# Down projection by seven half-size products, with the residual kept in DRAM

## The chip, the core and the metric

The kernel runs on one core of a Trainium2 chip. The metric is device time in microseconds (us), lower is better. Times shown are medians over several executions; the profile and the trace come from one execution of their own, in which the hardware profiler ran.

The core's engines each work through a queue of their own: TensorE (PE in the profile, its weight loads PEld), VectorE (DVE), ScalarE (ACT), GpSimd (POOL) and SyncE (SP). Here SP issues nearly all transfers between DRAM and the on-chip memory. TensorE writes its products to the eight banks of PSUM, from where VectorE and ScalarE fetch them.

## The reference

A transformer block with modulation: 2048 tokens of width 1024, 32 query heads over 4 key-value heads of 128, the last 512 cached keys, and a gated MLP of width 3584. All inputs are bfloat16.

```python
mod = (silu(c) @ w_mod).reshape(1, 6, 1, -1)
sa, ca, ga, sb, cb, gb = ...                     # six rows of mod
h = layernorm(x) * (1 + ca) + sa
x = x + ga * attention(h, k_cache[-512:], v_cache[-512:], wq, wo)
h = layernorm(x) * (1 + cb) + sb
x = x + gb * ((silu(h @ w_gate) * (h @ w_up)) @ w_down)
```

The last product, with `w_down` of 3584 x 1024, is the down projection. The sum in front of it is the residual.

## The kernel before

The attention works on four chunks of 512 tokens. In each chunk 32 heads are taken one by one; the query projection of a later head pair is done in seven products in place of eight (the same trick that the change uses below), its weight sums being kept in DRAM as `wq_sums` after the first chunk. A chunk ends with its output projection (`oproj`): 256 matmuls of 128x128 by 128x512 into all eight banks, in eight blocks of four heads. The weights of a block, 1 MB, lie in one of three buffers; `load_wo` loads a block's successor-but-two when the block is done. The last 64 matmuls finish the banks one after the other, and `add_to_x` (L678) multiplies each bank by the gate and adds it to `x_sb`, the residual, 32 KB in each partition and resident for the whole kernel. `oproj` calls `each` at fixed places; in the last chunk this runs pending work (the second norm, first sums of gate and up weights), in the others it does nothing.

The MLP works on two stretches of 1024 tokens (`NST`). In a stretch, 14 pairs (`NPR`) of 128-column tiles of F follow each other. `pair` (L987) makes gate and up for two tiles of F and two token halves in 14 products of four matmuls: `keep` copies a product from PSUM with ScalarE, `add` adds a later one to it with VectorE (L1003), `silu` runs on ScalarE and `times` (L1014) multiplies gate by up on VectorE. Between them `sums_of_pair` (through `tt_`, L540) makes the weight sums of the next pair, four for gate and four for up. The results lie in `gu`, 28 tiles of 1024 tokens.

Then `down` (L1067) runs twice, once for each half of the 1024 output columns: 8 token tiles x 28 tiles of F, 224 matmuls, into eight banks. Its weights come in pieces of 512 KB through six buffers (`load_wd`, issued by SP). Each finished bank goes through `add_to_x`, and `store` writes 128 KB of the output. During the first stretch's `down`, VectorE makes the norm of the second stretch, which SP transposes, and the sums of the normed input (`stretch_sums`). In the very last tile the columns are done in two parts of 256, so that only a small piece is left at the end.

Order on an engine is the order of the program. Buffers are tracked by `_Tracker`: an instruction waits on semaphores for the last writer and readers of what it touches, and `_Map.take` hands on these waits when a region of on-chip memory gets a new use. All places in the memory are written out by hand, in KB (`AT_X`, `AT_H`, ...).

Of the kernel before, what the change touches and what calls it, by code (L numbers as in the profile page):

```python
# [3 lines left out]
ALU = mybir.AluOpType  # L4
AF = mybir.ActivationFunctionType
BF16 = mybir.dt.bfloat16
# [112 lines left out]
def bass_adaLN_cond__sliding_block_cached__swiglu_ffn__prompt_kernel(  # L119
# [60 lines left out]
    x_sb = M.take(AT_X * KB, [NCH * TPC, D], BF16, BX)  # L180
# [71 lines left out]
    Q_last = [dq("q_last%d" % i) for i in range(1)]  # L252
# [6 lines left out]
    with nc.Block() as block:  # L259

        @block.gpsimd
        def _(g):
# [437 lines left out]

            def oproj(ch, first, each):
# [8 lines left out]
                for b_ in range(2, HG - 2):  # L710
                    for h in range(4 * b_, 4 * b_ + 4):
                        for k in range(TPC * HALF):
                            o_mm(ch, k, h)
                    load_wo(ch * HG + b_ + 3)
                    each()
                for k in range(TPC * HALF):
# [3 lines left out]
                    add_to_x(bank(o_bank(ch, k)), PB[o_bank(ch, k)], ga_bc, B_ga[hf], ch * TPC + tt, hf * 512, 512, k % 2)  # L720
# [35 lines left out]
            def mod_columns():  # L756

                while columns:
# [14 lines left out]
                    else:  # L773
                        T.op(DVE, lambda: V.tensor_copy(sb[:, 4 * hf:4 * hf + 4], bank(QBK, 4)), writes=PB[QBK] + [B_sb])

# [58 lines left out]
            for i in range(NA):  # L834
# [78 lines left out]
                if h == Hq - 1:  # L913
# [10 lines left out]
                    oproj(ch, o_start(ch), lambda: None)  # L924
# [5 lines left out]
            raw = [[M.take((144 + 8 * i + 4 * m) * KB, [DT, 256], BF16, [B_raw[i][m]]) for m in range(2)] for i in range(NRW)]  # L930
            Q_raw = [[dq("q_raw%d_%d" % (i, m)) for m in range(2)] for i in range(NRW)]
            B_ft = [bufs("ft%d_" % i, 4) for i in range(NTS)]
            ftq = [M.take((168 + 4 * i) * KB, [4, 4, P], F16, B_ft[i]) for i in range(NTS)]
# [3 lines left out]
            fn = [[M.take((180 + 4 * m + 2 * i) * KB, [CH], F32, [B_fn[m][i]]) for i in range(2)] for m in range(2)]  # L937
            B_gx, B_ux, B_sl = bufs("gx", 2), bufs("ux", 3), bufs("sl", 4)
            ux = [M.take((196 + i) * KB, [CH], F16, [B_ux[i]]) for i in range(3)]
            sl_ = [M.take((199 + i) * KB, [CH], F16, [B_sl[i]]) for i in range(4)]  # L940
# [46 lines left out]
            def pair(gp, order):  # L987

                p = gp % NPR
                f0, f1 = 2 * p, 2 * p + 1  # L990
# [22 lines left out]
                def times(f, half, u_, s_, bb=()):  # L1013
                    T.op(DVE, lambda: V.tensor_tensor(gu(f)[:, half * CH:(half + 1) * CH], u_[0], s_[0], ALU.mult),  # L1014
                         reads=[s_[1]] + [x for x in u_[1:]], writes=[B_gu[f]] + list(bb))

                keep(0, 1, 0)
                sums_of_pair(gp + 1, 0, 0)
                g_ = add(0, 2, one[0], 0)
                keep(1, 1, 0)  # L1020
                sl = silu(g_[0], [g_[1]], [])
                keep(0, 6, 1)
                sums_of_pair(gp + 1, 0, 1)
                u_ = add(1, 2, one[1], 0)
                times(f0, 0, u_, sl)
                keep(1, 6, 1)
                sums_of_pair(gp + 1, 0, 2)
# [175 lines left out]
```

## Time and profile before

| | |
|---|---|
| median of 9 runs | 1212.37 us (1211.81 to 1214.22) |
| the profiled execution | 1213.67 us, of which the span is 1211.9 us |
| ScalarE, copy of 128x512 float32 from PSUM (L996) | 168 of 596 ns |
| VectorE, addition from PSUM (L1003) | 168 of 689 ns |
| VectorE, gate times up, in on-chip memory (L1014) | 84 of 425 ns |
| VectorE, weight sums of 512 elements, bfloat16 and float16 in, float16 out (L540) | 224 of 418 ns |
| VectorE, gate times a bank of an output (L679) | 63 of 691 ns |
| DMA transposes | 159, median 4.3 us to landing |

The page of a profile lists the engines' busy time and its share of the span, then the span in 40 slices with a digit for each tenth of busy time, the granted TensorE clock (9 is full speed) and the DMA. "Chain" is the work that ended last, followed back from the end. Groups are instructions of one line and shape, with their number, their busy time and the mean of one. A timeline entry has start, duration, engine, line, operation, and in brackets the idle time before it and what ended that. L264 is the one line through which every matmul is issued.

### The profile page before, as it was taken

How to read it: one execution, taken by the hardware profiler on the slowest of the kernel's cores; microseconds unless marked ns; L12 is line 12 of the kernel's file. 1: busy time of each engine (PE TensorE's matmuls, PEld its weight loads, DVE VectorE, ACT ScalarE, POOL GpSimd, SP SyncE). 2: the span in 40 equal slices, each digit the busy share in tenths (PEclk: the TensorE clock that was granted, in tenths of full speed). 3: DMA queues.
4: the chain of work that ended last, by engine and by line, in shares of the span. 5: the costliest groups of instructions: out<-in, count | busy, mean ns of one | idle time of the engine just before them, and what ended most of it. 6: DMA issues, size and time to landing. Idle time of an engine off the chain costs nothing.

```text
span 1211.9 us, 20448 instructions
## 1 busy us (share of the span) xinstructions
PE 1188.8 (98%) x7941; PEld 687.9 (57%) x8074; DVE 712.3 (59%) x1568; ACT 474.2 (39%) x694; POOL 20.0 (2%) x41
## 2 busy tenths in 40 slices
PE   6999999999999999999999999999999999999999
PEld 4677646788457875478864444444444444444444
DVE  4888507887038873167643776777561677674023
ACT  4676403676016672056740344444000344443000
POOL 1000000000000000000000000000100000000000
PEclk9999999999999999999999999999999999999999
DMA  9999746998448986349948134433442323220221
GB/s 296 249 256 274 235 152 192 264 283 236 151 164 195 271 230 183 139 136 211 251 111 237 35 91 136 126 100 94 125 129 87 115 77 99 76 70 21 89 83 35
DMA packets 249824, 191.01 MB, mean 158 GB/s; under 512 B 107520, under 2 KB 225408, under 8 KB 245888
## 3 DMA queue, kind: packets, MB, share of 16 engines
q1 hardware_dynamic: 249712, 189.70, 55.7%
q8 instruction: 64, 1.05, 0.4%
q14 instruction: 32, 0.26, 0.1%
q10 hardware_dynamic: 16, 0.00, 0.0%
HBM read 152.57 MB, written 12.58 MB: 136 GB/s over the span
## 4 chain that ended last, share of the span: by engine, by line
PE 93%; DMA 2%; DVE 2%; SPq 1%; issue 1%; ACT 0%; POOL 0%; DVEq 0%
PE ps L264 93%; DMA arena<-arena 1%; DMA arena<-in_w_mod_dram 1%; SPq L283 1%; DMA arena<-in_A_wo_dram 0%; DVE arena L669 0%; SPq L946 0%; DVE arena L353 0%; DVE arena L747 0%; ACT arena L764 0%; DVE arena L601 0%; DVE arena L635 0%; DVE arena L668 0%; SPq L274 0%; SPq L370 0%
## 5 line engine op out<-in xcount | busy, mean ns | idle before, releaser
L264 PE MATMUL ps<-arena 128*128 128x512 bf16 (+5 forms) x7892 | 1185.9, 309 | 16.7 <-DMA arena<-in_w_mod_dram 4.8
L264 PEld LDWEIGHTS ps<-arena 128*128 128x128 bf16 (+1 forms) x8025 | 685.0, 98 | 517.0 <-issue 11.1
L652 ACT ACTIVATE arena<-ps 128x1024 bf16<-128x1024 f32 x256 | 249.7, 1021 | 39.6 <-PE ps L264 36.8
L996 ACT ACTIVATE arena<-ps 128x512 f32<-128x512 f32 x168 | 100.1, 596 | 282.9 <-PE ps L264 282.9
L679 DVE TENSOR_TENSOR arena<-ps,arena 128x512 bf16<-128x512 f32 (+1 forms) x65 | 44.4, 682 | 271.7 <-PE ps L264 271.5
L1003 DVE TENSOR_TENSOR arena<-ps,arena 128x512 f16<-128x512 f32 x168 | 115.8, 689 | 83.1 <-PE ps L264 80.3
L595 ACT ACTIVATE arena<-ps 128x256 f32<-128x256 f32 x134 | 51.3, 383 | 251.5 <-PE ps L264 250.7
L540 DVE TENSOR_TENSOR arena<-arena 128x512 f16<-128x512 bf16 (+2 forms) x288 | 132.0, 477 | 0.6
L669 DVE TENSOR_TENSOR arena<-ps,arena 128x512 bf16<-128x512 f32 x128 | 88.5, 692 | 4.7 <-DVE arena L668 0.2
L601 DVE TENSOR_TENSOR arena<-ps,arena 128x256 bf16<-128x256 f32 x180 | 75.7, 421 | 11.0 <-PE ps L264 6.3
L1010 ACT ACTIVATE arena<-arena 128x512 f16<-128x512 f16 x84 | 52.5, 625 | 27.8 <-DVE arena L1003 27.8
L668 DVE RECIPROCAL arena<-ps 128x4 f32<-128x4 f32 x128 | 23.1, 181 | 41.0 <-PE ps L264 40.3
L747 DVE SCALAR_TENSOR_TENSOR arena<-arena 128x512 f32<-128x512 bf16 x56 | 41.6, 743 | 0.1
L353 DVE BATCH_NORM_STATS2 arena<-arena 128x6 f32<-128x512 bf16 x60 | 41.2, 687 | 0.4
L1014 DVE TENSOR_TENSOR arena<-arena 128x512 bf16<-128x512 f16 x84 | 35.7, 425 | 9.2 <-DVE arena L1003 0.7
L360 POOL TENSOR_TENSOR arena<-arena 128x1 f32<-128x1 f32 x30 | 17.5, 583 | 867.3 <-DVE arena L358 865.0
L635 DVE CAST arena<-ps 128x256 bf16<-128x256 f32 x60 | 25.2, 420 | 10.2 <-PE ps L264 9.0
L681 DVE TENSOR_TENSOR arena<-arena 128x512 bf16<-128x512 bf16 (+1 forms) x65 | 27.3, 421 | 2.2
L597 DVE COPY arena<-ps 128x256 f32<-128x256 f32 x46 | 19.4, 422 | 13.7 <-PE ps L264 13.7
L364 DVE TENSOR_SCALAR arena<-arena 128x1024 bf16<-128x1024 bf16 x32 | 17.4, 543 | 13.9 <-DMA arena<-arena 8.3
L1014 DVE TENSOR_TENSOR arena<-ps,arena 128x512 bf16<-128x512 f32 x28 | 19.4, 692 | 7.9 <-PE ps L264 7.9
L374 DVE TENSOR_SCALAR arena<-arena 128x512 bf16<-128x512 bf16 x56 | 19.7, 408 | 6.4 <-DMA arena<-arena 6.4
(48 smaller groups left out, 79.9 us busy)
## 6 DMA issues: line engine op xcount, KB each, us to landing
arena<-in_A_wq_dram SPq DMA_DIRECT2D x64, 512.0 KB, 4.7
arena<-in_A_wo_dram SPq DMA_DIRECT2D x32, 1024.0 KB, 5.4
arena<-wq_sums SPq DMA_DIRECT2D x22, 1024.0 KB, 6.6
arena<-in_B_w_down_dram SPq DMA_DIRECT2D x29, 512.0 KB, 3.7
arena<-in_B_w_gate_dram SPq DMA_DIRECT2D x28, 512.0 KB, 3.7
arena<-in_B_w_up_dram SPq DMA_DIRECT2D x28, 512.0 KB, 4.7
arena<-in_w_mod_dram SPq DMA_DIRECT2D x8, 1024.0 KB, 7.7
wq_sums<-arena SPq DMA_DIRECT2D x8, 1024.0 KB, 5.5
```

The lines of the kernel that those rows point to most:

```text
L264: T.op(PE, lambda: TE.matmul(out_ap, lhsT, rhs, start=start, stop=stop, skip_group_check=loose), reads=reads, writes=bb)
L540: T.op(st, lambda: e.tensor_tensor(dst, x, y, op), reads=reads, writes=[dst_b])
L595: T.op(ACT, lambda: A.activation(sn[k], bank(QBK, 256), AF.Copy), writes=PB[QBK] + [B_sn[k]])
L601: T.op(DVE, lambda: V.tensor_tensor(dst, bank(XBK, 256, off), sn[k], ALU.add), reads=[B_sn[k]], writes=PB[XBK] + [B_q[i % NQ]])
L652: T.op(ACT, lambda: A.activation(ex[i % NEX][:, kt:kt + 2, :], bank(SCB[kt], 1024).rearrange("p (a b) -> p a b", a=2), AF.Exp, scale=att_s ...
L669: T.op(DVE, lambda: V.tensor_tensor(o_sb[i % NOS].rearrange("p (a b) -> p a b", a=TPC), num, rl_bc, ALU.mult), reads=[B_rl], writes=both + ...
L679: T.op(DVE, lambda: V.tensor_tensor(rt[s][:, 0:n], ps_ap, gate[:, lo:lo + n], ALU.mult), reads=[gate_b], writes=bb + [B_rt[s]])
L747: T.op(DVE, lambda: V.scalar_tensor_tensor(acc, ms[:, kc, :], sc[:, kc:kc + 1], acc, op0=ALU.mult, op1=ALU.add), reads=[B_ms, B_sc, B_acc] ...
L996: T.op(ACT, lambda: A.activation(fn[m][i], bank(b), AF.Copy), writes=PB[b] + [B_fn[m][i]])
L1003: T.op(DVE, lambda: V.tensor_tensor(ring[c_], bank(b), fn[m][i], ALU.add), reads=[B_fn[m][i]], writes=PB[b] + [bs[c_]])
L1010: T.op(ACT, lambda: A.activation(sl_[c_], src, AF.Silu), reads=reads, writes=writes + [B_sl[c_]])
L1014: T.op(DVE, lambda: V.tensor_tensor(gu(f)[:, half * CH:(half + 1) * CH], u_[0], s_[0], ALU.mult), reads=[s_[1]] + [x for x in u_[1:]], wri ...
```

## The change

Take a matrix A of 1024 tokens by 3584 and B, the weights, 3584 by 1024. A pair of token tiles (of which one belongs to the first and one to the second half of the stretch), a pair of tiles of F and the two halves of the output columns make a 2 x 2 product of blocks. It is now made with seven products of blocks instead of eight. For this, sums of blocks of A (`S1` to `S4`) are made in the pairs from the gate times up parts, in float16; sums of blocks of B (four for each of 14 row pairs) are made once, in the output projections of the first three chunks, and kept in DRAM as `wd_sums`. A product then runs over all 14 pairs of F and four token tiles, 56 matmuls, with its own 14 KB per partition of weights in one of two buffers. ScalarE issues these loads, and those and the stores of the weight sums.

Because the parts of A take more room than `gu`, the residual leaves the on-chip memory: after each output projection its 16 tiles are stored to DRAM (`x_mid`), read again for the norm of the second stretch (`ln_rows`), and again for the output in `down`. Several tiles have new places. The output is stored in whole rows of 1024, 256 KB each, and the split of the last tile is gone. `oproj` calls `each` after every head of its middle blocks, instead of after every block of four.

The core of the diff; places of buffers and the row loads are left out:

```diff
@@ def oproj(ch, first, each):
                     for h in range(4 * b_, 4 * b_ + 4):
                         for k in range(TPC * HALF):
                             o_mm(ch, k, h)
+                        each()
                     load_wo(ch * HG + b_ + 3)
-                    each()
...
+                    if hf:
+                        T.op(Q_x1[tt], lambda: SP.dma_start(x1_d[t * P:(t + 1) * P, :], x_sb[:, t, :]), reads=[BX[t]], writes=[B_x1[t]])
                     each()
...
+            def wd_sums(ch):
+                lo, hi = NP_ * ch // (NCH - 1), NP_ * (ch + 1) // (NCH - 1)
...
+                load(lo)
+                load(lo + 1)
+                for _ in range(6):
+                    yield
+                for r in range(lo, hi):
...
+                    for k in range(4):
+                        x, y, extra = ((b12, b11, []), (b22, t_[:, 0], [bt[0]]), (b22, b12, []), (b21, t_[:, 1], [bt[1]]))[k]
+                        tt_(DVE, V, t_[:, k], bt[k], x, y, ALU.subtract, [B_dr[r % 2]] + extra)
+                    T.op(Q_dk, lambda: A.dma_start(wd_t[:, :, r * 512:(r + 1) * 512].rearrange("k p n -> p k n"), dt_[r % 2]),
+                         reads=B_dt[r % 2], writes=[B_wdt[r]])
+                    load(r + 2)
+                    for _ in range(5):
+                        yield
...
-                    oproj(ch, o_start(ch), lambda: None)
+                    rounds = wd_sums(ch)
+                    oproj(ch, o_start(ch), lambda: next(rounds, None))
@@ def pair(gp, order):
+                def earlier(k):
+                    if p:
+                        down_sum(p - 1, k)
+
                 keep(0, 1, 0)
+                earlier(0)
                 sums_of_pair(gp + 1, 0, 0)
                 g_ = add(0, 2, one[0], 0)
                 keep(1, 1, 0)
                 sl = silu(g_[0], [g_[1]], [])
+                earlier(1)
                 keep(0, 6, 1)
                 sums_of_pair(gp + 1, 0, 1)
                 u_ = add(1, 2, one[1], 0)
-                times(f0, 0, u_, sl)
+                times("A11", u_, sl)
+                earlier(2)
                 keep(1, 6, 1)
                 sums_of_pair(gp + 1, 0, 2)
+                earlier(3)
                 keep(0, 5, 0)
...
+            def down_sum(p, k):
+                a_ = p % 2
+                one, x, y, op = ((("S1"), (a21[a_], B_a21[a_]), "A22", ALU.add), ("S2", "S1", "A11", ALU.subtract),
+                                 ("S3", "A11", (a21[a_], B_a21[a_]), ALU.subtract), ("S4", "A12", "S2", ALU.subtract))[k]
...
+            PROD = (("A11", "B11"), ("A12", "B21"), ("S2", 1), ("S1", 0), ("S3", 2), ("S4", "B22"), ("A22", 3))
...
+            def down(st, order, each):
...
+                for n, (a_, _) in enumerate(PROD):
+                    load_wd(n + 1)
...
+                    for k in range(4):
+                        b = (ab, cb)[n in (1, 4, 6)][k]
+                        for p in range(NPR):
+                            mm(bank(b), pt[a_][:, p, k * P:(k + 1) * P], wd[w_][:, p, :], p == 0 and n in (0, 1, 4), p == NPR - 1,
+                               [B_pt[a_][p], B_wd[w_][p // 7]], PB[b], loose=True)
+                            if p in ((3, 6, 9, 13) if n in (2, 3) else (6, 13)):
+                                each()
+                        if n in (0, 3):
+                            T.op(ACT, lambda: A.activation(u1[k], bank(b), AF.Copy), writes=PB[b] + [B_u1[k]])
+                        elif n == 2:
+                            T.op(ACT, lambda: A.activation(u2[k], bank(b), AF.Copy), writes=PB[b] + [B_u2[k]])
+                        else:
...
+                            if n != 5:
+                                T.op(DVE, lambda: V.tensor_tensor(u_, bank(b), u_, ALU.add), reads=[bu], writes=PB[b] + [bu])
+                                src, rd, wr = u_, [bu], []
+                            s_ = k % 2
+                            T.op(DVE, lambda: V.tensor_tensor(rt[s_], src, gb_bc[:, lo:lo + CH], ALU.mult),
+                                 reads=[B_gb[hf]] + rd, writes=wr + [B_rt[s_]])
+                            T.op(DVE, lambda: V.tensor_tensor(x_[:, lo:lo + CH], x_[:, lo:lo + CH], rt[s_], ALU.add),
+                                 reads=[B_rt[s_], bx], writes=[bx])
+                            if n >= 5:
+                                t = t0 + 4 * half + k
+                                T.op(Q_out[k], lambda: SP.dma_start(of[t * P:(t + 1) * P, :], x_), reads=[bx])
```

`load_wd` loads a product's weights in two halves of seven pairs, from `wd_sums` or straight from `w_down`; a matmul waits for its half. Product 0 of a stretch is loaded during its third pair. In the first stretch, `each` runs the norm of the second stretch from product 1 on and the `stretch_sums` in product 6.

## The prediction

> **What bounds the kernel now.** I read the page's busy times first, then its forty slices, then busy time by stage.
>
> ```profile
> PE 1188.8 (98%) x7941; PEld 687.9 (57%) x8074; DVE 712.3 (59%) x1568; ACT 474.2 (39%) x694; POOL 20.0 (2%) x41
> ...
> PEclk9999999999999999999999999999999999999999
> ...
> PE 93%; DMA 2%; DVE 2%; SPq 1%; issue 1%; ACT 0%; POOL 0%; DVEq 0%
> ```
>
> ```profile
> 140.00:196.00 56.00, 55.74 (x267) 25.85 (x270) 9.88 (x19) 0.90 (x1) 0.00 (x0) 1.00 0.51 174
> 185.00:190.00 5.00, 4.95 (x24) 2.28 (x24) 3.17 (x7) 0.00 (x0) 0.00 (x0) 1.00 1.00 358
> 675.00:844.00 169.00, 168.22 (x769) 76.62 (x783) 119.26 (x250) 79.07 (x139) 0.00 (x0) 1.00 0.34 100
> 844.00:942.00 98.00, 97.52 (x446) 44.42 (x455) 47.69 (x101) 1.22 (x2) 4.38 (x8) 1.00 0.40 115
> 1110.00:1212.00 102.00, 98.74 (x478) 47.48 (x486) 20.92 (x39) 1.12 (x2) 0.00 (x0) 1.00 0.20 66
> ```
>
> Stage rows give length, busy time of PE, PEld, DVE, ACT and POOL, granted clock, DMA share, GB/s. PE is busy 98%, at full clock, and is 93% of the chain: a matmul that is not issued shortens the kernel, if nothing else takes its place. The stages are an output projection (and five microseconds of it in which the DMA is full), the first 14 pairs, and the two down projections. The pairs repeat every 12.09 us (two like VectorE instructions stand at 691.43 and 703.52), which over 56 matmuls is 215.9 ns each. Fourteen pairs are 169.2 us. The first down projection lasts from about 846.3 to 943.0, 96.7 us for 448 matmuls, the same rate. Busy 309 ns per matmul on the page overlaps and is not the price.
>
> **What is removed.** Per stretch of 1024 tokens, 8 token tiles x 28 tiles of F x 2 halves = 448 matmuls become 7 products x 4 x 14 = 392. 2 x 56 x 215.9 ns = **24.2 us**, all on the path. The old last tile's split (56 matmuls of 256 columns for 28 of 512) is neutral: its stage takes 96.8 us of PE too.
>
> **Added VectorE work in the pairs.** Each pair gets four subtractions or additions of 512 16-bit elements. VectorE in a middle pair:
>
> ```profile
> 691.43 0.68 DVE L1003 TENSOR_TENSOR arena<-ps,arena 128x512 f16<-128x512 f32 x1
> 692.04 0.42 DVE L540 TENSOR_TENSOR arena<-arena 128x512 f16<-128x512 bf16 x1
> 693.84 0.69 DVE L1003 TENSOR_TENSOR arena<-ps,arena 128x512 f16<-128x512 f32 x1 [1.39 <-PE ps L264]
> 694.64 0.43 DVE L1014 TENSOR_TENSOR arena<-arena 128x512 bf16<-128x512 f16 x1
> 694.98 0.75 DVE L540 TENSOR_TENSOR arena<-arena 128x512 f16<-128x512 bf16 x2
> 696.43 0.69 DVE L1003 TENSOR_TENSOR arena<-ps,arena 128x512 f16<-128x512 f32 x1 [0.70 <-PE ps L264]
> ```
>
> Such an operation takes 0.42 alone and 0.335 back to back (0.75 for two); mixed float16 and bfloat16 operands are in these rows. VectorE goes from 119.26/14 = 8.5 to about 9.9 us of 12.09. Place matters more than the sum. One lands before the addition at 691.43 and makes it 0.34 late; the second comes after it and leaves about 0.7 of the idle 1.39. The third and fourth come before 696.43: 0.67 into an idle 0.70. So each is absorbed before the next addition, and TensorE returns to those banks four products (3.5 us) later. Cost **0**; at double price, 0.67 each, the addition at 696.43 is 0.65 late, still inside that 3.5 us.
>
> **Added in the first three output projections.** 14 rounds of four subtractions, 56 x 0.42 = 24 us over three stages, where VectorE is busy 9.88 of 56 us. Its next work there, the residual addition, starts 43 us in, after the rounds. ScalarE issues their transfers; its next activation belongs to the next chunk. Five rounds move 5 x (0.5 + 0.5) MB: 9.7 MB becomes 15 MB, 267 GB/s. The danger is the weight load of the projection itself. It is issued two blocks, 13.8 us, ahead and lands in 5.4; at half the bandwidth it needs about 9. Cost 0; bounds 0 and 3 x 1.5. The 16 residual rows stored from SP wait for the last addition, and the head transposes and summed query weights of the next chunk queue behind them by about 1.6 us (1.1 of addition, 0.5 of issue); those are needed groups of heads later. In the last projection the pending work is called four times as often, so its 17 VectorE items end before the residual additions instead of among them: no PE wait stands there to gain.
>
> **The new weight loads** are the real risk. A product lasts 56 x 215.9 ns = 12.09 us and reads 1792 KB (1.84 MB); the next one's load starts when the product before has ended. Rows for their price:
>
> ```profile
> q1 hardware_dynamic: 249712, 189.70, 55.7%
> ...
> arena<-in_A_wo_dram SPq DMA_DIRECT2D x32, 1024.0 KB, 5.4
> ...
> arena<-in_B_w_down_dram SPq DMA_DIRECT2D x29, 512.0 KB, 3.7
> ```
>
> Capacity is 358 GB/s at a DMA share of 1.00 (the stage row 185 to 190). Alone, 1.84 MB takes 5.1 us plus about 2 of latency (1 MB in 5.4 is 2.9 + 2.5). ScalarE issues after its last copy of the product before (0.6) and two issues of 0.4 (SP needs 0.37 to 0.39 for such a one): the second half lands about 8.5 us in; its first matmul comes at 12.09 + 7 x 0.216 = 13.6. So the second stretch waits for nothing. In the first, SP adds 3 MB in products 1 to 3: eight residual rows for the output, eight for the next norm and their transposes. The old trace cannot show two loaded rings: q1 holds nearly all bytes. Here the Trainium skill speaks against the change ("DMA: Bandwidth & Descriptors", "Issuing engines are not separate DMA queues"): transfers from ScalarE and SP run on the same 16 engines, which by "Queues, rings and completion order" take turns between the rings. Were the ring separate, the wait is 0. By the rule ScalarE's gets half while SP has work: 1.84 MB at 179 GB/s is 10.3, with issue and latency 13.3, against 13.6. Turns are by packet, of unlike size here, so I take 1 us in all, with bounds 0 and 3 x 2.
>
> **Smaller costs.** (a) Tail. Now the last matmul is followed by 0.42 + 0.29 and a 64 KB store:
>
> ```profile
> 1209.25 0.42 DVE L679 TENSOR_TENSOR arena<-ps,arena 128x256 bf16<-128x256 f32 x1 [2.12 <-PE ps L264]
> 1209.71 0.29 DVE L681 TENSOR_TENSOR arena<-arena 128x256 bf16<-128x256 bf16 x1
> ```
>
> Then: 0.69 (float32 sum from PSUM), 0.68 (the float32-bfloat16 row at L752 has 684 ns), 0.42, 1.1 more, and a 256 KB store, 0.4 more by the loads' slope. **+1.5**. (b) Turn from the first down projection to the pairs. In its last product VectorE has per tile 1.87 (three chained) + 2 x 0.69 (stretch sums) = 3.25 us against 3.02 of matmuls; it ends some 0.7 late, so the first addition of the pair starts about 1 us late, and the silu behind it holds ScalarE's copy that the seventh product needs. **+0.5**, bounds 0 and 1.5. (c) ScalarE issues two loads inside a pair, twice: 0.8 before a copy with 0.9 of room: **+0.1**. Other evictions hide under 3 us of matmuls per tile.
>
> **Sum.** -24.2 + 1.5 + 0.5 + 0.1 + 1.0 = -21.1. The profiled execution took 1213.67 (span 1211.9 and 1.8 around it): 1192.6. It lies 1.3 above the median of the runs, 1212.37, so the same saving gives 1191.3 there; I predict **1191.5**.
>
> **Rivals.**
> 1. *Loads late in the whole first down projection*: six waits of 1 to 2 us add 5 to 11 in place of 1, **1196 to 1202**. For: rows, transposes and weights together need about 300 GB/s. Against: this holds in two or three products. Chance 0.14.
> 2. *VectorE bounds the pairs*: were mixed operands as slow as PSUM ones (0.69) and the additions stacked, about 0.3 us per pair, 28 times, 8 us: **1199**. Against: the mixed rows above. Chance 0.05.
> 3. *Slower than before*: weights from ScalarE's ring arrive late at every product. Twelve of fourteen loads can be waited for, and 22.7 us of net saving over 12 is 1.9 us each: the second half would have to land 15.5 us in, 1.84 MB at about 140 GB/s after issue and latency. From there it decides; at 130 GB/s each wait is 3.0 us, and 1190.3 (the sum without its load term) + 36 gives **1226**. Longer waits would cost twice: "TensorE: Matmul & The Clock Gate" (Part 1) has the clock halved after idle windows of about 3.4 us. This trace has no such gap (all slices at 9) and can't show it. At 120 GB/s a wait is 4.2 us: 1241 at the row's full clock, by the rule up to 1.7 more each, 1261. For: the bandwidth of that ring is unmeasured here. Against: 512 KB in 1 KB pieces lands in 3.7 from SP. Chance 0.06.
> 4. *The change does not do what it says* (different matmul rate for these operands, or no fewer matmuls): about **1212**. The pairs already mix these types at 215.9 ns. Chance 0.02.
>
> **Numbers.** The sum's case has the remaining 0.73, 1188.5 to 1195.5: bounds of the loads and the turn on top, and -2.6 if loads, turn and part of the tail cost nothing. To leave out no more than 2 in 10 the range goes up into rivals 1 and 2: 1188 to 1200. A measurement tells 0.2% from no change, 2.4 us. Faster: the sum, rivals 1 and 2: 0.92; same 0.02; slower 0.06.
>
> **What will show it.** The two down stages should be about 84.6 us each, the matmul count lower by 140 (112, and the 28 of the split); the pairs still 12.09 apart with VectorE near 9.9 busy; output projections still 55 to 56. TensorE waits on the new weight tiles at products 2 to 4 of the first down projection would size the load term; waits there in the second, or in the pairs on VectorE, make the prediction wrong.

## The result and the profile after

The changed kernel takes 1192.43 us, the median of 10 executions; the kernel before takes 1212.59 us, the median of 31. The ratio is 0.9839 (95% interval 0.9829 to 0.9849). The profiled execution took 1192.46 us with a span of 1190.7; The forecast was 1191.5 for the median, in a range of 1188 to 1200, and for the profiled execution 1192.6, with a span 21.1 shorter than before's.

One thing the median doesn't show: three of the ten executions of the changed kernel lie at 1197.86, 1197.92 and 1208.74 us, whereas the kernel before stayed between 1211.5 and 1214.7 in more than sixty executions. Without those three the median is 1192.3.

The page's busy times, clock and chain, in the order of before:

```profile
PE 1164.0 (98%) x7810; PEld 673.8 (57%) x7934; DVE 786.9 (66%) x1758; ACT 488.4 (41%) x718; POOL 20.0 (2%) x41
...
PEclk9999999999999999999999999999999999999999
...
PE 94%; DMA 2%; DVE 2%; issue 1%; SPq 1%; ACT 0%
```

TensorE is still the bound, at full clock, with 140 fewer weight loads into it, the forecast number (of the matmuls 131 fewer are recorded; a few records are missing). VectorE has gained 75 us of work and the chain doesn't show it. Busy time by stage, columns as before (length, PE, PEld, DVE, ACT, POOL, clock, DMA share, GB/s): an output projection, the first 14 pairs, the first down projection, two stretches inside that one, and the second down projection.

```profile
140.00:196.00 56.00, 55.74 (x258) 25.53 (x262) 16.05 (x34) 0.19 (x1) 0.00 (x0) 1.00 0.69 241
675.00:844.00 169.00, 168.21 (x770) 76.62 (x783) 137.07 (x302) 79.66 (x139) 0.00 (x0) 1.00 0.33 95
844.00:930.00 86.00, 85.75 (x396) 38.77 (x398) 52.22 (x111) 7.81 (x14) 4.38 (x8) 1.00 0.78 229
880.00:892.00 12.00, 12.00 (x58) 5.36 (x57) 5.76 (x14) 2.30 (x5) 1.64 (x3) 1.00 1.07 274
892.00:904.00 12.00, 12.00 (x57) 5.48 (x56) 6.17 (x15) 0.74 (x2) 1.64 (x3) 1.00 1.02 224
1099.00:1191.00 92.00, 87.13 (x400) 39.42 (x403) 30.75 (x54) 8.39 (x14) 0.00 (x0) 1.00 0.46 166
```

The first three rows have TensorE as full as before: 55.74 of 56, 168.21 of 169, 85.75 of 86. In the down projection the DMA share has gone from 0.40 to 0.78, and for 24 us it stands at 1.02 to 1.07 while only 224 to 274 GB/s are moved, where five microseconds of before gave 358 at 1.00. (The share adds up the times of all packets, so that it can pass 1.) The DMA is occupied there by something other than bytes.

TensorE's waits, with total, number and longest, include one that is new:

```profile
PE ps L265 <- ACT arena L1045: 1.6, 1, 1.6
```

It is at the turn from the first down projection to the second stretch's pairs. Five lines of that place in time order, ScalarE, VectorE and TensorE together (start, duration, engine, line; in brackets the idle time before and what ended it):

```profile
933.57 0.68 DVE L1298 TENSOR_TENSOR arena<-ps,arena 128x512 f32<-128x512 f32 x1
...
935.70 0.68 DVE L1052 TENSOR_TENSOR arena<-ps,arena 128x512 f16<-128x512 f32 x1
...
936.41 0.63 ACT L1059 ACTIVATE arena<-arena 128x512 f16<-128x512 f16 x1 [2.40 <-DVE arena L1052]
936.95 1.06 ACT L1045 ACTIVATE arena<-ps 128x512 f32<-128x512 f32 x2
...
937.59 2.76 PE L265 MATMUL ps<-arena 128*128 128x512 f16 x12 [1.62 <-ACT arena L1045]
```

VectorE comes to the last bank of the down projection at 933.57, too late; the pair's first addition (L1052) follows at 935.70, the silu waits 2.40 us for it, the copy (L1045) stands behind the silu, and TensorE waits 1.62 us for the copy's bank. That is the path which the prediction drew, three times as long.

Term by term, in the profiled executions:

| term | forecast | measured |
|---|---|---|
| 112 matmuls fewer | -24.2 | -12.1 and -12.0 |
| weight loads of the down projections | +1.0 | +0.2 (one wait, 0.5 on PEld) |
| turn | +0.5 | +1.6 |
| tail, last eviction to the span's end | +1.5 | +1.6 (2.65 to 4.27) |
| VectorE in the pairs, rounds in the output projections | 0 | 0 |
| a third and fourth issue of ScalarE in a pair | +0.1 | not to be told apart |
| up to the start of the MLP | none | -0.6 (not the change's, see below) |

The marks are the first copy (ScalarE) of each stretch's pairs and the eviction of the very last bank. From the first to the second mark it was 265.91 us and is 254.04, so -11.87. A late load is contained in this: from the last copy of product 0 (858.09) to the first eviction of product 1 (861.39) it is 3.30 us, in the second profile of the same kernel (below) 3.09, so the wait on PEld cost TensorE 0.2, and without it the saving is 12.08. From the second to the third it was 265.11 and is 254.74, so -10.37, in which the 1.62 of the turn are contained: -11.99 without them. With -0.58 ahead of the MLP and +1.62 behind the last eviction this is -21.2, the difference of the spans. Each stretch gains its 56 matmuls of 215.9 ns (12.09), and next to nothing is given back inside it.

The 0.58 ahead of the MLP belongs to the two executions and not to the change. In before's profile the granted clock falls to half for some microseconds near the start (stage row as above), where the changed kernel's has 1.00:

```profile
26.00:28.00 2.00, 2.00 (x6) 0.65 (x5) 2.00 (x9) 1.84 (x3) 0.00 (x0) 0.50 0.37 79
```

Two variants below, alike up to this point, also have 0.50 in this row of their profiles (the tail alone, the weights by SP), and they reach the first mark at 678.32 and 678.26 us, where before has 678.23. A digit of the page stands for 30 us and reads 9 there; that is why the prediction held that before's trace has no drop of the clock. It has one.

### The profile page after: what moved, and what is told of

Same layout as the page of the kernel before. It is cut to its first block, busy times and chain, and to the rows that moved or that the text cites. A ratio compares the mean times of both kernels' runs of the same rounds, so it can differ in the third digit from the quotient of the medians.

```text
span 1190.7 us, 20519 instructions
## 1 busy us (share of the span) xinstructions
PE 1164.0 (98%) x7810; PEld 673.8 (57%) x7934; DVE 786.9 (66%) x1758; ACT 488.4 (41%) x718; POOL 20.0 (2%) x41
## 3 DMA queue, kind: packets, MB, share of 16 engines
q8 instruction: 62, 1.02, 0.3%
## 4 chain that ended last, share of the span: by engine, by line
PE 94%; DMA 2%; DVE 2%; issue 1%; SPq 1%; ACT 0%
PE ps L265 94%; DMA arena<-in_w_mod_dram 1%; SPq L284 1%; DMA arena<-in_A_wo_dram 1%; DVE arena L670 0%; DVE arena L755 0%; ACT arena L772 0%; DVE arena L602 0%; DMA arena<-arena 0%; DVE arena L636 0%; DVE arena L669 0%; SPq L275 0%; DVE arena L541 0%; SPq L299 0%; PE ps L269 0%
## 5 line engine op out<-in xcount | busy, mean ns | idle before, releaser
L265 PE MATMUL ps<-arena 128*128 128x512 bf16 (+5 forms) x7761 | 1161.0, 309 | 18.6 <-DMA arena<-in_w_mod_dram 5.0
L265 PEld LDWEIGHTS ps<-arena 128*128 128x128 bf16 (+1 forms) x7885 | 670.5, 98 | 508.2 <-issue 11.4
L541 DVE TENSOR_TENSOR arena<-arena 128x512 f16<-128x512 bf16 (+1 forms) x456 | 191.3, 456 | 49.0 <-DMA arena<-in_B_w_down_dram 47.8
L1045 ACT ACTIVATE arena<-ps 128x512 f32<-128x512 f32 x168 | 99.9, 595 | 221.2 <-PE ps L265 221.2
L1052 DVE TENSOR_TENSOR arena<-ps,arena 128x512 f16<-128x512 f32 x168 | 115.8, 689 | 48.3 <-PE ps L265 44.9
L670 DVE TENSOR_TENSOR arena<-ps,arena 128x512 bf16<-128x512 f32 x128 | 88.5, 692 | 4.9 <-DVE arena L669 0.5
L602 DVE TENSOR_TENSOR arena<-ps,arena 128x256 bf16<-128x256 f32 x180 | 75.7, 421 | 11.3 <-PE ps L265 6.8
L680 DVE TENSOR_TENSOR arena<-ps,arena 128x512 bf16<-128x512 f32 x32 | 22.1, 692 | 82.2 <-PE ps L265 82.2
L1298 DVE TENSOR_TENSOR arena<-ps,arena 128x512 f32<-128x512 f32 x24 | 16.5, 688 | 62.1 <-PE ps L265 62.1
L636 DVE CAST arena<-ps 128x256 bf16<-128x256 f32 x60 | 25.2, 420 | 10.3 <-PE ps L265 8.9
L354 DVE BATCH_NORM_STATS2 arena<-arena 128x6 f32<-128x512 bf16 x44 | 30.2, 686 | 0.2
L1288 ACT ACTIVATE arena<-ps 128x512 f32<-128x512 f32 x16 | 9.6, 597 | 40.7 <-PE ps L265 40.7
L1064 DVE TENSOR_TENSOR arena<-ps,arena 128x512 bf16<-128x512 f32 x28 | 19.4, 692 | 6.7 <-PE ps L265 6.6
L1059 ACT ACTIVATE arena<-ps 128x512 f16<-128x512 f32 x28 | 16.7, 597 | 17.1 <-PE ps L265 17.1
```

The costliest lines, as they stand in the source:

```text
L265: T.op(PE, lambda: TE.matmul(out_ap, lhsT, rhs, start=start, stop=stop, skip_group_check=loose), reads=reads, writes=bb)
L354: T.op(DVE, lambda: V.bn_stats(st_sb[i][:, 6 * hf:6 * hf + 6], x_sb[:, t, 512 * hf:512 * hf + 512]), reads=[BX[t]], writes=[B_st[i]])
L541: T.op(st, lambda: e.tensor_tensor(dst, x, y, op), reads=reads, writes=[dst_b])
L602: T.op(DVE, lambda: V.tensor_tensor(dst, bank(XBK, 256, off), sn[k], ALU.add), reads=[B_sn[k]], writes=PB[XBK] + [B_q[i % NQ]])
L670: T.op(DVE, lambda: V.tensor_tensor(o_sb[i % NOS].rearrange("p (a b) -> p a b", a=TPC), num, rl_bc, ALU.mult), reads=[B_rl], writes=both + ...
L1045: T.op(ACT, lambda: A.activation(fn[m][i], bank(b), AF.Copy), writes=PB[b] + [B_fn[m][i]])
```

## The experiments

All times are beside the kernel before, run on the same chip. Three questions: are the zero terms really free, what sets the turn's wait, and how near are the loads to their deadlines?

### The same kernel again, and the turn relieved

> The changed kernel as it is, to see its spread and a second profile. My account: 1192.4 us (1190.7 to 1194), one wait of 1.6 us of TensorE at the turn from the first down projection to the pairs, no wait for weights above 0.5 us. If the executions of 1198 and 1209 us among the ten before belong to the kernel, because its first down projection leaves the weight loads no reserve, about 2 in 10 executions lie 5 us or more above the median again; if they were chance, none do.

1190.99 us (1189.8 to 1201.43), 0.9835 [0.9809, 0.9861]. Its profile has no wait of ScalarE's copy at the turn: the first stretch and its down projection take 253.82, exactly one product less than 265.91. So 1.62 is one draw of the turn's wait and 0 is another. One of the six executions, 1201.43, lies 10 us above the median.

> Four of the eight stretch sums (fs2, fs3) move from product 6 of the first down projection into the first pair of the second stretch. My theory: the wait of 1.62 us at the turn is VectorE's backlog, 2.8 us of sums in the way of the evictions; without them the first addition of the pair starts on time and the wait goes: 1190.8 us. Rival: the wait is set by ScalarE's or PSUM's own order, not by VectorE's backlog: 1192.4, wait unchanged.

Half of the stretch sums go from the last product into the first pair, which needs them only later:

```diff
+                    elif gp and k in (1, 2):
+                        stretch_sums(k + 1, 0)
+                        stretch_sums(k + 1, 1)
...
-                        todo.extend(lambda k=k, j=j: stretch_sums(k, j) for k in range(4) for j in range(2))
+                        todo.extend(lambda k=k, j=j: stretch_sums(k, j) for k in range(2) for j in range(2))
```

1190.33 us (1189.43 to 1200.33), 0.9824 [0.98, 0.9848], and no wait at the turn. As the unaltered kernel had none in its second profile either, the missing wait alone shows nothing; the time that VectorE had for its work does, in the table below. The balance of the last product, on which the forecast of 0.5 rested, can't be the whole cause, since the wait comes and goes with the same product. What VectorE had done before the turn differs from one execution to the next; in the first profile of the changed kernel it had stood still for transposes:

```profile
891.55 0.55 DVE L1338 TENSOR_SCALAR arena<-arena 128x1024 bf16<-128x1024 bf16 x1 [3.85 <-DMA arena<-arena]
...
905.05 0.55 DVE L1338 TENSOR_SCALAR arena<-arena 128x1024 bf16<-128x1024 bf16 x1 [5.25 <-DMA arena<-arena]
```

These are the norm's own steps of row tiles (L1338): each writes a buffer that the transpose of an earlier tile has to have read. The later the norm ends, the more is left for the last product.

### Where the norm's time goes

> Residual rows 0 to 3 are loaded from the middle of product 0 on, rows 4 to 7 in product 3 in place of product 1; nothing else changes. My theory: the backlog at the turn comes from the norm being late, since its row loads and transposes queue behind these rows; with 1 MB less ahead of them the norm ends earlier and the wait at the turn falls from 1.6 to about 0.5 us: 1191.3, and executions far above the median become rarer. Rival: the backlog is the balance of product 6 alone (3.1 us of VectorE against 3.02 of matmuls per tile): the wait stays at 1.6, 1192.4.

The rows for the output are loaded half a product later, and in product 3 in place of product 1, to leave the DMA to norm and weights:

```diff
...
-                    if n == 1:
+                    if n == 3:
                         for k in range(4):
                             xr[4 + k] = load_rows(Q_xr[k], t0 + 4 + k, 6 + 2 * k)
...
```

1191.25 us, 0.9821 [0.9808, 0.9833]. VectorE no longer waits for the norm's rows (5.4 us before), but the wait for transposes becomes 13.9 us where it was 10.5. Measured against the pairs that follow it, the norm ends between where the two profiles of the unaltered kernel have it. What was saved at one wait was paid at the next: the forecast time came, but not for the forecast reason.

> The eight residual rows of each stretch's output are issued by ScalarE behind the weights of product 1 and 2, so that SP's ring holds only the rows of the norm and its transposes. My theory: the wait at the turn and the rare long executions come from the norm of the second stretch, late because its rows and transposes stand behind these rows; now VectorE's wait for the first norm row (5.4 us) goes, the norm ends 4 us or more earlier, no wait at the turn, no execution 5 us above the median: 1190 to 1191.5. Rival (the transposes themselves are slow whatever stands before them, or the weights of product 1, 8 to 14 us to landing, get later): wait at the turn as before, or new waits for weights, 1191.5 and above.

The output's rows are issued by ScalarE, behind the first weights, instead of by SP ahead of the norm:

```diff
-            Q_xr = [dq("q_xr%d" % i) for i in range(4)]
+            Q_xr = [dq("q_xr%d" % i, A) for i in range(4)]
...
```

1190.33 us, 0.9819 [0.9806, 0.9833]. Again the row wait is gone and transposes are waited for instead, 14.1 us. One of five executions took 1207.9, so SP's rows aren't what makes single executions long.

> The eight transposes of the second stretch's norm are left out (so the second stretch works on the normed input of the first, and half of the output is another one); all other loads, waits and operations stay. My theory: the transposes, moving at the same time as the weights of products 3 and 4, are what makes the norm late and the weights of those products slow. Without them the last scaling ends 18 us or more before the pairs resume (16.0 in the profile of the change), TensorE has no wait at the turn, these weights land within 8 us, and all executions lie within 3 us: 1190 to 1191.5. Rival (the long executions come from elsewhere): one in five or so still lies 5 us or more above the median.

The eight transposes of the second norm are left out; the second stretch, half of the output, is then not computed from the normed input. All else is issued as before.

```diff
-                        if turn is not None:
-                            ln_turn(*turn)
...
-                ln_turn(*turn)
```

1190.17 us, 0.9816 [0.9803, 0.983]. The two 12 us stretches from above, and the whole down projection:

```profile
880.00:892.00 12.00, 12.00 (x58) 5.46 (x56) 8.93 (x21) 2.39 (x4) 2.20 (x4) 1.00 0.68 242
892.00:904.00 12.00, 12.00 (x57) 5.42 (x56) 10.40 (x27) 0.60 (x1) 1.10 (x2) 1.00 0.45 153
844.00:930.00 86.00, 85.79 (x396) 39.01 (x399) 55.28 (x114) 7.79 (x13) 4.39 (x8) 1.00 0.60 208
```

This is the DMA's hidden occupant. Over the 86 us its share falls from 0.78 to 0.60, which is 15.5 us of all DMA engines, and the rate from 229 to 208 GB/s, which is 1.8 MB; at the plain rate of 358 GB/s those would take 5.0 us. So a transposed byte costs some three times a plain one here, an estimate from these rows. Without the transposes the norm runs at VectorE's pace, with no wait for the DMA after its first rows, and its last scaling is at 907.0 instead of 916.5. The weights issued from 882 to 895 us land within 4.7 to 7.4 us, against 5.5 to 11.2. None of five executions was long; at one in five that happens one time in three by chance, so it doesn't settle what makes them long.

With these profiles the turn's wait can be set against its cause. "Room" is the time from the start of the norm's last scaling (L375) to the first copy of the second stretch's pairs; all rows have the stretch sums where the change put them.

| kernel | room, us | TensorE's wait at the turn, us |
|---|---|---|
| weights by SP (below) | 26.2 | 0 |
| transposes left out | 24.2 | 0 |
| tail alone (below) | 17.1 | 0 |
| the same again | 17.0 | 0 |
| pair sums doubled (below) | 16.6 | under 0.2 (none listed) |
| output rows by ScalarE | 16.6 | 0.2 |
| rounds doubled (below) | 16.3 | 0.5 |
| output rows later | 16.1 | 0.7 |
| the changed kernel, first profile | 15.2 | 1.6 |
| flooded (below) | 8.5 | 7.3 |

From 17 downward each microsecond of room lost is nearly one of waiting: by this table VectorE needs some 17 us for what it has to do after the norm, and the transposes decide how much it gets. The moved stretch sums fit in. The trial with them had a room of 15.1 and no wait, where the changed kernel with 15.2 waited 1.6. A later kernel with them (the tail and the moved sums together) had a room of 11.3, for which a line between the last two rows gives 4.9 us, and waited 2.8. Four sums of 0.69 are 2.8 us less to do, a little more than the difference of 2.1. These are two profiles, but they say what the times could not: VectorE's work in the last product and the end of the norm set the wait together.

### How near the weight loads are to their deadlines

> In products 2 to 5 of the second stretch's down projection SP issues twelve idle loads of 256 KB each per product into memory that is free there, on six queues; 3.1 MB beside the product's own 1.84 MB, more than 12.09 us can carry at 358 GB/s. The result is unchanged. My theory (engines taking turns between the two rings, so ScalarE's ring keeps half): the weights land about 10 to 13 us after their issue, TensorE waits at most 1 us per product, 4 in all: 1191 to 1195. Rival (the ring with more work takes more): landings of 15 us and more, waits of 2 us or more per product, 1199 and above; then SP's traffic is what could turn the change slower.

In products 2 to 5 of the *second* down projection, SP gets 12 idle loads of 256 KB per product, into free memory:

```diff
...
+                        if st == NST - 1 and 2 <= n <= 5:
+                            for j in range(3):
+                                i = (3 * k + j) % 6
+                                load_rows(Q_fl[i], 3 * k + j, (0, 2, 4, 22, 24, 26)[i])
```

1199.09 us, 0.9881 [0.9846, 0.9917], spread from 1192.94 to 1214.59; the profiled execution is that longest one. Three executions lie at 1192.9 to 1195.1, as the theory had it, and three at 1203.1 and above, as the rival had it, so the time decides nothing. TensorE's longest waits in the trace:

```profile
PE ps L265 <- ACT arena L1045: 7.3, 1, 7.3
PE ps L265 <- DMA arena<-in_B_w_down_dram: 6.2, 3, 5.2
PE ps L265 <- DMA arena<-wd_sums: 4.2, 1, 4.2
```

Only the second row belongs to the flood (5.9 of it). There, weight sums, stored in runs of 7 KB, land 8.0 to 12.5 us after issue, median 10.3, and nothing waits for them; the halves of the block taken straight from `w_down`, in runs of 1 KB, need 12.4 and 18.8, and TensorE waits 0.6 and 5.2 for them. In bytes, ScalarE's queue moved 4.27 of 8.34 MB in 1135 to 1160 us, where its loads have long runs, and 2.21 of 6.80 in 1160 to 1180, where most have short ones. So it got about its half for long runs and less for short ones: that is compatible with the rule of the Trainium skill ("DMA: Bandwidth & Descriptors", "Queues, rings and completion order") which the prediction weighed, since that section has the rings take turns by packet. That the length of a run is what makes the difference is a reading: no run changed it alone, and this is one execution.

The other two rows are in the *first* down projection, which the edit doesn't touch: that part went badly in this execution by itself, and it is the only such trace.

```profile
880.00:892.00 12.00, 12.00 (x58) 5.43 (x56) 4.42 (x11) 2.39 (x4) 1.64 (x3) 1.00 1.04 192
892.00:904.00 12.00, 7.84 (x29) 3.05 (x28) 2.60 (x6) 0.60 (x1) 0.55 (x1) 0.86 1.14 136
```

At a share of 1.04 and 1.14 only 192 and 136 GB/s are moved. Weights issued at 882.6 land 17.3 us later (7.7 in the first profile) and TensorE waits 4.2; the norm waits 11.5 us for one transpose; the turn then costs 7.3. After each of the two waits the granted clock drops (0.86 in the row above, 0.87 in 930 to 950). What the Trainium skill ("TensorE: Matmul & The Clock Gate", Part 1) says of idle windows of about 3.4 us is seen here with waits of 4.2 and 7.3: such a wait costs more than itself. A long wait isn't the only way to it: before's trace has its 0.50 at 26 to 28 us after waits of at most 0.34 us each, among short matmuls that left TensorE busy for 1.20 of 2 us (22 to 24). No run here varied this.

> The weights of the down projection are issued by SP instead of ScalarE, nothing else. My theory: a second ring is part of what hides these loads; on SP's they stand in line behind residual rows and transposes that wait for VectorE, so in the first stretch products 2 to 5 wait 1 to 4 us each: 1196 to 1206, the second stretch unchanged. Rival (the ring doesn't matter, all transfers share the same engines anyway): 1190 to 1193.

The same loads, issued by SP in its order instead of by ScalarE:

```diff
-            Q_wd = [[dq("q_wd%d_%d" % (i, j), A) for j in range(2)] for i in range(NWD)]
+            Q_wd = [[dq("q_wd%d_%d" % (i, j)) for j in range(2)] for i in range(NWD)]
...
-                    T.op(Q_wd[i][j], lambda: A.dma_start(dst, src), reads=rd, writes=[B_wd[i][j]])
+                    T.op(Q_wd[i][j], lambda: SP.dma_start(dst, src), reads=rd, writes=[B_wd[i][j]])
```

1197.71 us (1196.65 to 1199.44), 0.9875 [0.986, 0.9889]. All of it is in the first stretch, 261.47 us against 253.82 in the second profile of the changed kernel; the second stretch is unchanged. It is one long wait, for product 4, and not the several that were forecast. SP and TensorE in product 3 and at the start of product 4:

```profile
890.33 3.80 SPq L371 DMA_TRANSPOSE arena<-arena  x2
894.24 1.00 SPq L1246 DMA_DIRECT2D arena<-wd_sums  x2
...
899.46 45.84 PE L265 MATMUL ps<-arena 128*128 128x512 f16 x195 [4.08 <-DVE arena L375]
```

The weights stand in SP's queue behind transposes, each of which waits for VectorE, and are issued at 894.24 where ScalarE issued them at 882.5. The first half lands 5.1 us later, at 899.3, and TensorE starts at 899.46. The bracket names VectorE's scaling of the norm, which only happened to end then. The loads themselves were no slower (median 6.7 us, against 7.6); what the second queue buys isn't bandwidth but a place of its own in line. What the wait does to the clock is seen best in rows of 1 us:

```profile
899.00:900.00 1.00, 0.54 (x2) 0.28 (x3) 1.00 (x4) 0.00 (x0) 0.00 (x0) 0.50 1.05 373
...
906.00:907.00 1.00, 1.00 (x7) 0.46 (x5) 0.97 (x2) 0.00 (x0) 0.00 (x0) 1.00 1.04 367
```

TensorE starts again at half the clock, 0.50 up to 905, and is back at 1.00 from 906 on: about 6 us at half speed, which cost about 3.0 (an estimate from these rows). The wait of 4.08, the clock and a wait of 0.29 for product 1 make 7.4 of the 7.65.

### Are the free parts free?

> Each of the four sums that the change adds to a pair is made twice: 28 x 4 more operations of 0.34 to 0.42 us on VectorE, 41 us in all. My theory (the room in the pairs absorbs even the double price): pairs still 12.09 us apart, 1192.4 to 1193. Rival (VectorE near its limit becomes the bound): 0.3 us or more per pair, 1200 and above.

Each of the four sums of a pair is made twice:

```diff
-                tt_(DVE, V, pt[one][:, p, :], B_pt[one][p], x[0], y[0], op, [x[1], y[1]])
+                for _ in range(2):
+                    tt_(DVE, V, pt[one][:, p, :], B_pt[one][p], x[0], y[0], op, [x[1], y[1]])
```

1192.11 us (1189.79 to 1192.27), 0.9821 [0.9808, 0.9834].

```profile
675.00:844.00 169.00, 168.26 (x770) 76.60 (x783) 155.10 (x353) 81.34 (x138) 0.00 (x0) 1.00 0.33 95
```

VectorE is now busy 155.1 of 169 us, and its idle time ahead of the additions falls from 48.3 to 7.4 us in all pairs, yet the first stretch takes 253.89 against 253.82. The sums are free, and would be at twice the price.

> Each round of the weight sums in the first three output projections loads its rows twice and stores its sums twice: 10 MB per projection in place of 5, about 360 GB/s with the projection's own weights. My theory (the rounds' traffic hides with some room): single traffic costs nothing, double makes loads of the projection's weights land later than their 13.8 us at places, 0 to 6 us in all: 1191 to 1197. Rival (the rare executions of 1198 to 1209 come from this stage, which is at its limit already): 1200 and above, with waits of TensorE for the projection's weights.

In the output projections each round of weight sums loads twice and stores twice, with the same arithmetic:

```diff
...
-                load(lo)
-                load(lo + 1)
+                for r in (lo, lo, lo + 1, lo + 1):
+                    load(r)
...
+                    for q_ in (Q_dk, Q_dk2):
+                        T.op(q_, lambda: A.dma_start(wd_t[:, :, r * 512:(r + 1) * 512].rearrange("k p n -> p k n"), dt_[r % 2]),
+                             reads=B_dt[r % 2], writes=[B_wdt[r]])
+                    load(r + 2)
```

1210.93 us (11 executions), 0.9987 [0.9975, 1.0]: nearly the whole gain is gone, and not through the projection's own weights, which were the danger in the prediction. TensorE's waits (total, number, longest):

```profile
PE ps L265 <- DVE arena L680: 13.7, 10, 3.6
```

Four links of the chain in the second projection (start, length, what):

```profile
326.23 6.10 DMA wd_sums<-arena
332.76 7.27 DMA arena<-in_B_w_down_dram
340.47 6.15 DMA wd_sums<-arena
347.06 5.34 DMA arena<-in_B_w_down_dram
```

Loads into one buffer, and stores out of it, wait for one another, so that doubled transfers stretch the rounds, 5 us apart in the mean in the changed kernel, to 11 to 14 us. The last round then ends at 358, and the residual addition (L680), which has to empty TensorE's banks, stands behind it on VectorE: it starts at 357.97 where the changed kernel has 345.34. There the last round ended at 326.04, with 19.3 us to spare. The third projection goes the same way. This profile's span is 18.4 us longer than the changed kernel's: 13.7 are the waits, and for the rest there is the clock, which is at 0.50 after both groups of waits (362 to 370 and 536 to 542 us). The price of zero was right, but what covers it is that the rounds end long before the residual additions, not bandwidth.

### Towards a better version

> The changed kernel with the shorter tail alone: the known part of the output goes through the gate in product 4 of the last stretch, product 6 leaves one multiplication, one addition and 128 KB per tile. Theory: from the last matmul to the end 3.3 us instead of 4.3, 1190.2 to 1191.4. Rival: the tail is the store's latency alone, unchanged: 1191.5 and above.

The last product's other addend is multiplied and added ahead of time, and half of the row is stored early. In the last stretch:

```diff
-                            if n != 5:
+                            early = st == NST - 1
+                            if n != 5 and not (n == 6 and early):
...
+                            if n == 4 and early:
+                                T.op(DVE, lambda: V.tensor_tensor(rt[s_], u2[k], gb_bc[:, 0:CH], ALU.mult),
+                                     reads=[B_gb[0], B_u2[k]], writes=[B_rt[s_]])
...
```

1192.58 us (1189.85 to 1202.3), 0.9852 [0.9821, 0.9883]. From the last eviction to the end the profile has 3.4 us in place of 4.3, as the missing 0.69 and the half-size store should give; in the time it is lost in the spread.

> The moved stretch sums, and a shorter tail: in the last stretch the part of the output that is known after product 2 is multiplied by the gate and added to the rows during product 4, their other half is stored then, and product 6 leaves one multiplication, one addition and a 128 KB store per tile. Theory: tail shorter by 0.7 of VectorE and 0.3 of the store, turn at zero: 1189.5 to 1190.5, about 1 below the kernel with the moved sums alone. Rival (the added VectorE work or stores in product 4 get in the way): 1191 or more.

The tail and the moved stretch sums together: 1189.88 us (1188.49 to 1191.87), 0.9812 [0.9799, 0.9825], the lowest median of all. Its profile caught the norm late (last scaling 919.5), and the turn cost 2.8 in spite of the moved sums.

> Rows on ScalarE's ring, moved stretch sums and the shorter tail together. Theory: 1189.0 to 1190.0, no wait of TensorE at the turn, last matmul to end 3.3 us. Rival (the moved sums stand before the second addition of the pair and hold it when the norm is late): a wait at the turn remains, 1190.5 and above.

These two and the rows by ScalarE: 1190.73 us (1189.42 to 1193.86), 0.9823 [0.9809, 0.9837]; no wait at the turn, one of 0.8 on weights. The three intervals overlap with each other. That of the tail with the moved sums ends at 0.9825, just below the 0.9829 where the changed kernel's begins, but inside that of its second set (0.9809 to 0.9861); about a microsecond may be there, but these runs don't prove it.

## Why the prediction was right, point by point

**The bound and the saving.** TensorE's 215.9 ns per matmul is the price, and the two stretches gave 12.1 and 12.0 us for their 56 matmuls, once the late load and the turn are set apart. As next to nothing that was added got in front of TensorE inside a stretch, the saving arrived whole.

**VectorE in the pairs.** 9.8 us of a pair against a forecast of 9.9, pairs still 12.09 apart. Reading the place of each sum, and not the total alone, was what carried the zero; the doubling shows that even the double price, which the prediction had put inside the banks' 3.5 us, was right.

**Output projections.** Zero, as forecast; 241 GB/s where 267 were expected (the projection shown has four of the 14 rounds, the forecast counted five). The prediction saw the two covers, the lead of the weights' loads and the end of the rounds well before the residual additions, but named only the first as the danger. Doubling the transfers broke the second.

**Weight loads.** 1.0 was set, 0.2 came; here the first profile was the mild end. The one wait was for product 1, not for products 2 to 4: its halves, in runs of 1 KB, landed 8.4 and 13.9 us after issue. The forecast of two or three products with rows, transposes and weights at once was right in kind, but the DMA is fullest in products 3 and 4 (880 to 904), later than expected, and the forecast counted the transposes as bytes. They cost more than that, and in the flooded kernel's execution the bound of 3 x 2 was about used up by one wait of 4.2 and its clock. Two sums of this part are off: with the 3.4 us of issue and latency of the sum before it, the load at half the bandwidth lands at 13.7, not 13.3, so it had nothing to spare against 13.6; and the net saving that rival 3 has to eat up is 22.1 by the prediction's own terms, not 22.7. Neither moves the 1191.5.

**The turn.** The path was right (VectorE late, addition, silu, copy, matmul), the size a term to mend: 1.6 in one profile, 0 in the next, 7.3 in a bad one. The 0.5 was worked out from the last product alone, with VectorE level at its beginning; it begins behind when transposes hold up the norm.

**The tail.** +1.6 for +1.5.

The two mis-sized terms, +1.0 and +0.5 against +0.2 and +1.6, nearly cancel, and the 0.6 ahead of the MLP, which is a matter of the two executions, takes up the rest: part of the agreement of 1192.46 with 1192.6 is luck. The turn's 1.62 even passes its upper bound of 1.5, which knew nothing of the norm. No rival happened as a median. The first one's mechanism, loads late in the first down projection, does happen in single executions, and it was the loads from SP that came nearest to it: 1197.7 inside its 1196 to 1202.

What stays open: the long executions. By their mean granted clock, 0.994 to 0.997 in the changed kernel's where its others have 0.998 to 1.0, TensorE ran at less than full clock in them for a while, as it does after long waits. They were seen in the changed kernel and in five of its variants, never in the kernel before; the one with a trace (flooded) has late weights and slow transposes at a DMA share above 1. That the others are of the same kind was not tried, nor why transposes are slower in one execution than in another, nor transposes spread apart in time as before's were.

## What to carry to other kernels

Work taken off the bounding engine is worth its full price if each added instruction ends before the next fetch from PSUM that the bounding engine waits for, so put the gaps of the trace in order of time and don't only add them up. On an engine that works in order, look for an instruction that itself waits and stands ahead of a PSUM fetch or of a load that is needed soon: the turn, the doubled rounds and the weights on SP all lost time in this way, and only the turn had too much compute as a second cause. A load that must be on time wants a queue with nothing waiting in it. And a few microseconds of TensorE's waiting can cost as much again in clock.

## What the runs showed of the hardware that was not expected

- Transposes fill the DMA engines without moving much: in 880 to 892 and 892 to 904 us the share is 0.88 to 1.15 at 136 to 283 GB/s in the profiles that have them there beside plain loads, 0.68 and 0.45 at 242 and 153 GB/s in the one that leaves them out.
- Under load from another queue (one execution), 896 KB in 7 KB runs landed in 8.0 to 12.5 us and in 1 KB runs in 12.4 and 18.8.
- After a wait of 4.08 us TensorE ran at a clock of 0.50 for about 6 us; in the 12 to 20 us around waits of 4.1 to 7.3 us the mean was 0.78 to 0.87. At the start of before the clock was 0.50 for a while after waits of no more than 0.34 us.
- A wait's named releaser can be a bystander: 4.08 us were put down to VectorE when a load that had been issued 5.2 us earlier landed.
